# Weights of layer 2 in a ring of 12 entries, and the groups of layer 1's Strassen rounds in pairs

## The chip, the cores and the metric

The kernel runs on one core of a Trainium2 chip. The metric is device time in microseconds of one execution, the median of several runs. The engines are named as the profile names them: PE (matrix multiply) with its weight loads PEld, DVE (VectorE), ACT (ScalarE), POOL (GpSimd) and SP (SyncE, which here only issues DMAs, in program order, from one queue).

## The reference

Three stages follow one another: a masked linear attention with decay ("retention"), a first feed-forward layer with the activation mish, and a second one with a sigmoid form of gelu. The weights arrive in float64.

```python
ret = scores * Dmat[None, :, :, :]          # scores = q k^T / sqrt(64), Dmat: gamma ** (i - j), lower triangle
attn_out = np.matmul(ret, v)                # 4 batches, 8 heads, 576 positions, 64 wide
x = attn_out.transpose(0, 2, 1, 3).reshape(2304, 512)
h = x @ w_in                                # 512 x 2048
x = (h * np.tanh(softplus(h))) @ w_out      # layer 1: mish, 2048 x 512
h = x @ moe2_w_in
x = (h / (1.0 + np.exp(-1.702 * h))) @ moe2_w_out   # layer 2
```

## The kernel before

**Numbers.** Each float32 operand of a product is split into a high part that PE multiplies in one pass and a rest, and three products (high by high, high by rest, rest by high: `PARTS`) are added in PSUM. Weights arrive as float64 and are rebuilt with integer operations on DVE, ACT and POOL.

**Stages.** X holds the 2304 tokens as 512 x 2304 (four pieces of 128 partitions, 9 KB each). The attention fills X. `first_layer` works on blocks of 768 tokens: the first block (512 + 256 tokens) plainly, blocks 1 and 2 (`R_ROUNDS`) by Strassen's scheme in its up product (7 products instead of 8 of 2 x 2 quarters) and plainly in its down product. `second_layer` works on the three blocks (s = 0, 1, 2) with Strassen's scheme in both products. For one block of layer 2 there are 56 steps up (8 groups r of hidden units, 7 products each, `L645`) and 56 steps down (7 products, 8 r each, `L692`). A step is six matmuls of 128 x 384 columns.

**The weights of layer 2.** Before use, seven combinations of a quarter's weights are formed and written to DRAM, as the tensor `stream`. This is `prepare`: it loads a quarter's float64 words (`cr<-w_dram`), rebuilds and combines them in steps that are laid between PE's steps, and writes `stream<-cy` (`L328`). There are 32 preparations: 14 and 13 of them in the two Strassen blocks of layer 1, and the last five (j = 27 to 31, "late") in the first 56 steps of layer 2. Layer 2 then reads `stream` back, 112 steps for each of three blocks, 256 KB a step, into a ring of buffers:

```python
RING = [("w0", 4)] + [(f"x{k}", 2) for k in range(2)]
```

So the ring has one piece of 4 steps (w0, one DMA of 1 MB) and two of 2 steps (x0, x1, one DMA of 512 KB each): 8 entries. `load_weights(j + 2)` stands at the first step of piece j, on SP. The buffer that it fills is that of piece j - 1, so SP waits there until PE has done with piece j - 1. The buffers x2 and x3 hold the words of the late preparations, and temporaries (`t3` in x3, `u4` in x2).

**Operands of the down product.** For step i + 3 the function `operand`, called in step i, has ACT copy a piece to its high part and DVE subtract the rest, into a tile `g2`. Of four steps one used the buffer "side", the others a ring of 3 under the name "g", so four operands exist at a time.

**A Strassen round of layer 1.** Group r of a block is a list of 15 places, `R_STEPS`. At a number, PE does the six matmuls (`L1099`) of that product; at `None` it does one piece of the down product of the group before (`L1036`: `drawn`, 3 matmuls of 512 and 3 of 256 columns, one of four output pieces e). Products 1, 6, 5 and 3 use PSUM bank A, and 2, 7 and 4 bank E; ACT and DVE read a bank between two products (`pre`, `plus`), form mish and split the result (`high`, `low`). At each place, moved-on steps of the preparations under way are issued (`position`). 16 rounds are done. The ring here (`first_ring`) has the same shape, w0, x0, x1, and reads `first_stream` (`L981`).

**What sets the order.** `tc.manual_schedule()` keeps the written order on each engine. Every engine works off its own list in order, and waits on semaphores.

Of the kernel before, what the change touches and what calls it, by code (L numbers as in the profile page):

```python
# [82 lines left out]
R_STEPS = (1, None, 2, None, 6, None, 7, None, 5, None, None, 3, None, 4, None)  # L83
# [17 lines left out]
def retention_mish_gelu_kernel(ctx: ExitStack, tc: tile.TileContext, qkv, w1, w2, first_unit, rests, out):  # L101
# [55 lines left out]
    prepared = set()  # L157
    temp = []
# [115 lines left out]
    def prepare(j, r, part, half):  # L274
# [4 lines left out]
        raw = keep.tile([P, 4, P], I64, tag=f"x{2 + j % 2}", name="cr")  # L279
# [46 lines left out]
        yield from pause(2)  # L326
# [6 lines left out]
        yield from pause(2)  # L333
# [122 lines left out]
    def x_parts(s, t3_in=None):  # L456
# [3 lines left out]
        t3 = (place(t3_in) if t3_in else keep).tile([P, 2, TH], F32, tag=f"w{t3_in}" if t3_in else "x3", name="t3")  # L460
# [11 lines left out]
    def x_ops_in_turn(s, minus, t3_in=None):  # L472
# [6 lines left out]
        for jobs in (  # L479
            (lambda: high(1, x11), lambda: tt(nc.vector, t3, x22, x12, ALU.subtract)),  # L480
            (lambda: low(1, x11), lambda: high(2, x21)),
            (lambda: tt(nc.vector, x12, x12, x11, ALU.subtract),),
            (lambda: low(2, x21),),
            (lambda: tt(nc.vector, x11, t3, x11, ALU.add), lambda: high(6, x11)),
            (t_4, lambda: high(7, t3)),
            (lambda: low(6, x11),),
# [4 lines left out]
            (lambda: low(3, x22),),  # L491
            (lambda: high(4, x21),),
# [39 lines left out]
    RING = [("w0", 4)] + [(f"x{k}", 2) for k in range(2)]  # L532
# [51 lines left out]
    def second_layer():  # L584
# [12 lines left out]
        ops = {}  # L597

        def operand(i):
# [23 lines left out]
        for s in range(N_ROUND):  # L623
# [45 lines left out]
            assert len(prepared) == 4 * NR and not under_way  # L669
            extra = {}  # L670
# [30 lines left out]
            for n_p, p in enumerate(DOWN_ORDER):  # L701
# [21 lines left out]
                for e in range(2):  # L723
# [262 lines left out]
    def first_layer():  # L986
# [35 lines left out]
        pieces += [old(n - 3, range(NK))] + [old(n - 2, (e,)) for e in range(NK)] + [old(n - 1, (e, e + 1)) for e in (0, 2)]  # L1022
# [3 lines left out]
        def drawn(g, m, e, base):  # L1026
            def piece():
                if m == 0 and e == 0:
# [5 lines left out]
                for t, (o, w) in enumerate(BLOCKS):  # L1034
                    for a, b in PARTS:
                        nc.tensor.matmul(  # L1036
                            acc[t, e][:, :w],
                            lhsT=W[1, m // 2][:, m % 2, a, e * P : (e + 1) * P],
                            rhs=g[:, b, o : o + w],
# [4 lines left out]
                if m == NM - 1:  # L1044
                    for t, (o, w) in enumerate(BLOCKS):
                        evacuate(e, t, base + o)
# [3 lines left out]
        for n_s, s in enumerate(R_ROUNDS):  # L1050
            base = two(s)[0].start
            for r in range(NR):
# [30 lines left out]
                for n_e, p in enumerate(R_STEPS):  # L1083
                    if p is None:
                        if pieces:
                            pieces.pop(0)()
# [142 lines left out]
```

## Time and profile before

| | |
|---|---|
| median of 3 runs | 875.09 us (873.03 to 880.24) |
| the profiled execution | 875.2 us, of which 873.5 us lie between first and last instruction |
| PE busy | 821.9 us (94%) |
| PEld, DVE, ACT, POOL busy | 766.0, 608.9, 455.7, 110.4 us |
| DMA | 219.67 MB, mean 251 GB/s |
| layer 2 on PE | 465.4 to 869.9 us |

The span runs from the first instruction to the last one; 1.7 us of the execution lie around it. Busy time of PE counts each matmul to its modelled end, though the next one begins before that, so a PE that is busy 94% still has idle time that is to be found in the views of waits, chains and stretches.

### The profile page before, as it was taken

Reading aid. Unit: us, or ns where it says so; the run is one execution under the profiler, and the core shown is the slowest. Engines: PE = TensorE matmul, PEld = TensorE weight load, DVE = VectorE, ACT = ScalarE, POOL = GpSimd, SP = SyncE. Lnnn points to the kernel's source line nnn. Section 1 sums busy time; section 2 is a strip of 40 time slices with the busy share of each in tenths; the row PEclk is TensorE's granted clock in tenths of the full one; section 3 lists DMA queues with packets and bytes.
Section 4 is the critical chain, followed back from the end, with each engine's and each line's share of the span. In section 5 each row is a group of like instructions: output and inputs, shape, how many; then the busy total and the mean of one; then the engine's idle time right before and its main releaser. Section 6 shows DMA issues by size and latency. Waiting matters only on the chain.

```text
span 873.5 us, 14230 instructions
## 1 busy us (share of the span) xinstructions
PE 821.9 (94%) x5392; PEld 766.0 (88%) x5392; DVE 608.9 (70%) x1118; ACT 455.7 (52%) x861; POOL 110.4 (13%) x124
## 2 busy tenths in 40 slices
PE   8999999999999999998999889899889998999987
PEld 8898888888998999988999789898889988989987
DVE  4887999987767676676564676886345886445675
ACT  5446777757666566565563444652224563224542
POOL 3542322311221201221100110000000000000000
PEclk9999999999999999999999999999999999999999
DMA  9965668747979866979744788768576677676675
GB/s 365 424 280 178 227 212 253 253 142 256 342 256 350 289 201 207 311 261 319 279 143 163 290 314 277 247 227 269 195 243 214 219 260 266 202 249 224 209 265 178
DMA packets 84117, 219.67 MB, mean 251 GB/s; under 512 B 5584, under 2 KB 51664, under 8 KB 74960
## 3 DMA queue, kind: packets, MB, share of 16 engines
q1 hardware_dynamic: 83904, 218.56, 72.1%
q8 instruction: 43, 0.70, 0.3%
q14 instruction: 26, 0.21, 0.1%
q10 hardware_dynamic: 144, 0.20, 0.1%
HBM read 169.98 MB, written 48.76 MB: 250 GB/s over the span
## 4 chain that ended last, share of the span: by engine, by line
PE 58%; DMA 30%; DVE 4%; ACT 3%; issue 3%; POOL 1%; SPq 0%; POOLq 0%; DVEq 0%; ACTq 0%
DMA ring<-stream 22%; PE p L645 12%; PE p L692 11%; PE acc L1036 10%; PE p L1099 8%; PE h L389 8%; PE acc L410 7%; DMA unit<-qkv_dram 2%; DMA cr<-w_dram 2%; DMA ring<-first_stream 2%; DMA stream<-cy 2%; PE o L896 1%; PE sc L834 1%; PE o L885 1%; ACT c L122 1%
## 5 line engine op out<-in xcount | busy, mean ns | idle before, releaser
L645 PE MATMUL p<-xop,ring 128*128 128x384 f32 x1008 | 185.2, 342 | 21.9 <-DMA ring<-stream 21.1
L645 PEld LDWEIGHTS p<-xop,ring 128*128 128x128 f32 x1008 | 178.5, 192 | 28.3 <-DMA ring<-stream 13.5
L692 PE MATMUL p<-g,ring 128*128 128x384 f32 x1008 | 180.5, 336 | 17.0 <-DMA ring<-stream 16.3
L692 PEld LDWEIGHTS p<-g,ring 128*128 128x128 f32 x1008 | 173.9, 188 | 23.6 <-ACT g L122 16.5
L1036 PE MATMUL acc<-g,w 128*128 128x512 f32 (+1 forms) x768 | 152.1, 338 | 0.0
L1036 PEld LDWEIGHTS acc<-g,w 128*128 128x128 f32 x768 | 130.3, 188 | 18.3 <-ACT X L122 0.6
L1099 PE MATMUL p<-xop,ring 128*128 128x384 f32 x672 | 139.1, 342 | 4.7 <-DMA ring<-first_stream 3.7
L122 ACT ACTIVATE g<-cs 128x384 fp32r<-128x384 f32 x168 | 88.2, 525 | 83.7 <-PE p L692 83.6
L448 DVE TENSOR_TENSOR g<-cs,g 128x384 fp32r<-128x384 f32 x168 | 93.6, 557 | 45.5 <-ACT g L122 44.6
L1099 PEld LDWEIGHTS p<-xop,ring 128*128 128x128 f32 x672 | 114.1, 189 | 7.3 <-ACT cy L122 3.0
L122 ACT ACTIVATE cs<-cs 128x384 f32<-128x384 f32 x72 | 37.8, 524 | 128.8 <-DVE cs L448 125.3
L206 POOL TENSOR_TENSOR cy<-cr 128x256 int32<-128x256 int32 x64 | 48.2, 773 | 284.5 <-DVE cr L202 108.7
L410 PE MATMUL acc<-g,w 128*128 128x512 f32 (+1 forms) x384 | 72.6, 337 | 0.0
L410 PEld LDWEIGHTS acc<-g,w 128*128 128x128 f32 x384 | 60.3, 190 | 7.6
L448 DVE TENSOR_TENSOR g<-c,g 128x384 fp32r<-128x384 f32 x64 | 36.1, 567 | 41.7 <-ACT g L122 41.3
L122 ACT ACTIVATE g<-c 128x384 fp32r<-128x384 f32 (+1 forms) x96 | 50.3, 524 | 12.4 <-PE acc L410 10.3
L448 DVE TENSOR_TENSOR cs<-cs 128x384 f32<-128x384 f32 x96 | 54.0, 562 | 0.8
L206 POOL TENSOR_TENSOR raw<-raw 128x512 int32<-128x512 int32 x32 | 38.0, 1187 | 101.3 <-DVE raw L202 84.0
L122 ACT ACTIVATE raw<-raw 128x512 int32<-128x512 uint32 x64 | 41.8, 679 | 14.1 <-DVE raw L190 14.0
L122 ACT ACTIVATE cr<-cr 128x512 int32<-128x512 uint32 x64 | 42.0, 670 | 13.2 <-DMA cr<-w_dram 11.1
L122 ACT ACTIVATE c<-c 128x384 f32<-128x384 f32 x48 | 25.1, 524 | 41.9 <-DVE c L448 41.7
L122 ACT ACTIVATE c<-p 128x384 f32<-128x384 f32 x64 | 30.9, 483 | 29.8 <-PE p L1099 29.6
(79 smaller groups left out, 925.5 us busy)
## 6 DMA issues: line engine op xcount, KB each, us to landing
ring<-stream SPq DMA_DIRECT2D x42, 1024.0 KB, 4.8
ring<-stream SPq DMA_DIRECT2D x84, 512.0 KB, 4.5
stream<-cy SPq DMA_DIRECT2D x32, 896.0 KB, 5.3
raw<-w_dram SPq DMA_DIRECT2D x32, 512.0 KB, 7.9
cr<-w_dram SPq DMA_DIRECT2D x32, 512.0 KB, 5.1
unit<-qkv_dram SPq DMA_DIRECT2D x15, 1024.0 KB, 10.6
ring<-first_stream SPq DMA_DIRECT2D x14, 1024.0 KB, 6.7
ring<-first_stream SPq DMA_DIRECT2D x28, 512.0 KB, 6.0
```

The costliest lines, as they stand in the source:

```text
L122: nc.scalar.activation(out=o, in_=i, func=f, scale=scale, bias=bias)
L206: nc.gpsimd.tensor_tensor(out=o, in0=upper, in1=bits, op=ALU.add)
L389: nc.tensor.matmul(h[:, :n], lhsT=W[0, m // 2][:, m % 2, a, k * P : (k + 1) * P], rhs=xs[t, k][:, b, :n], start=((k, a, b) == order[0]), s ...
L410: nc.tensor.matmul(acc[t, e][:, :n], lhsT=W[1, m // 2][:, m % 2, a, e * P : (e + 1) * P], rhs=g[:, b, :n],  start=(begins(i) and a == 0 an ...
L448: eng.tensor_tensor(out=o, in0=a, in1=b, op=op)
L645: nc.tensor.matmul(banks[p], lhsT=w[:, k, a * P : (a + 1) * P], rhs=x[:, b, k], start=(p not in SAME and k == 0 and a == 0 and b == 0), st ...
L692: nc.tensor.matmul(banks[e, p], lhsT=w[:, e, a * P : (a + 1) * P], rhs=g[:, b], start=(p != 2 and r == 0 and a == 0 and b == 0), stop=(r = ...
L834: nc.tensor.matmul(sc[j][:n, p, :n], lhsT=kt[sl, p, :], rhs=qt[sl, p, :], start=True, stop=True)
L885: nc.tensor.matmul(o[sl, p, :n], lhsT=before[:, p, sl], rhs=qt[:, p, :], start=(p == 0), stop=True, skip_group_check=True,)
L896: nc.tensor.matmul(o[sl, p, :n], lhsT=v[:n, p * P + 64 * j : p * P + 64 * j + 64], rhs=pm[u][j][:n, p, :n], start=(c == 0 and p == 0), sto ...
L1036: nc.tensor.matmul(acc[t, e][:, :w], lhsT=W[1, m // 2][:, m % 2, a, e * P : (e + 1) * P], rhs=g[:, b, o : o + w], start=(m == 0 and a == 0 ...
L1099: nc.tensor.matmul(bank, lhsT=w[:, a, k * P : (k + 1) * P], rhs=x[:, b, k], start=(p in (1, 2, 7) and k == 0 and a == 0 and b == 0), stop= ...
```

## The change

It has five parts.

1. The ring of layer 2 takes x2 and x3 as well: pieces of 4, 2, 2, 2, 2 steps, 12 entries. `load_weights(j + 4)` stands at the first step of piece j; four pieces are loaded ahead of layer 2.
2. The words of the late preparations go into a tile `raws` of two halves in the buffer "side"; after the up steps of block 0 that buffer holds `t3` and `u4` (`spare`). In every preparation the write to `stream` stands one place later, and the place after it, where its buffer counts as free, one earlier.
3. The operands of the down product lie in pairs in the three buffers "g": six at a time.
4. `R_STEPS` puts the products of a round together in pairs, and a down piece takes two output pieces e: 6 matmuls of 512 columns, then 6 of 256. An empty place issues nothing on PE.
5. The steps of ACT and DVE in a round, and those that form the operands of the next block, are moved to fit.

```diff
-R_STEPS = (1, None, 2, None, 6, None, 7, None, 5, None, None, 3, None, 4, None)
+R_STEPS = (1, "down", "", 2, 6, "down", "", 7, 5, "down", "", 3, 4, "down", "")
...
+    spare, raws = [], []
...
-        raw = keep.tile([P, 4, P], I64, tag=f"x{2 + j % 2}", name="cr")
+        if j == sum(PREPARED_IN[:2]):
+            raws.append(keep.tile([P, 2, 4, P], I64, tag="side", name="raws"))
+        raw = raws[0][:, j % 2] if raws else keep.tile([P, 4, P], I64, tag=f"x{2 + j % 2}", name="cr")
         nc.sync.dma_start(out=raw, in_=w2[r, part, half])
...
-        yield from pause(2)
+        yield from pause(3)
         c, step = (r * NP, 1) if part == 0 else (UP_STEPS + r, NR)
         nc.sync.dma_start(
             out=stream[:, c : c + (NP - 1) * step + 1 : step, half],
...
-        yield from pause(2)
+        yield "skip"
         live["cy"] -= 1
...
+        if spare:
+            t3 = spare[0][:, :2]
...
-    RING = [("w0", 4)] + [(f"x{k}", 2) for k in range(2)]
+    RING = [("w0", 4)] + [(f"x{k}", 2) for k in range(NK)]
...
-            if i % 4:
-                g = keep.tile([P, 2, TH], F32R, tag="g", name="g2", bufs=LAG)
-            else:
-                g = keep.tile([P, 2, TH], F32R, tag="side", name="g2")
-            ops[i] = g
+            if c == UP_STEPS or i % 2 == 0:
+                twos[0] = keep.tile([P, 2, 2, TH], F32R, tag="g", name="g2", bufs=LAG)
+            g = ops[i] = twos[0][:, i % 2]
...
+            if s == 0:
+                spare.append(keep.tile([P, 4, TH], F32, tag="side", name="spare"))
...
-                            sums["u4"] = keep.tile([P, 2, TH], F32, tag="x2", name="u4")
+                            sums["u4"] = spare[0][:, 2:]
...
-        def drawn(g, m, e, base):
+        def drawn(g, m, es, base):
...
+                    for e in es:
+                        for a, b in PARTS:
+                            nc.tensor.matmul(
+                                acc[t, e][:, :w],
...
-                    elif n_e == 2:
+                    elif n_e == 3:
                         plus(11, E)
...
-                    pieces += [drawn(g_[h], 2 * r + h, e, base) for e in range(NK)]
+                    pieces += [drawn(g_[h], 2 * r + h, (e, e + 1), base) for e in (0, 2)]
```

On SP, at the start of layer 2, a load of 128x2048 is a w0 piece (4 steps), one of 128x1024 an x piece (2 steps). Ahead of the words of the first late preparation (`cr`, later `raws`) stand, before:

```order
L549 DMA ring<-stream 128x2048
L549 DMA ring<-stream 128x1024 x2
L280 DMA cr<-w_dram 128x512
L549 DMA ring<-stream 128x2048
L549 DMA ring<-stream 128x1024
L280 DMA cr<-w_dram 128x512
```

There three pieces of the ring (8 entries) come first. On the same queue at the same place, changed:

```order
L554 DMA ring<-stream 128x2048
L554 DMA ring<-stream 128x1024 x4
L283 DMA raws<-w_dram 128x512
L554 DMA ring<-stream 128x2048
L554 DMA ring<-stream 128x1024
L283 DMA raws<-w_dram 128x512
```

In the second list all five pieces stand ahead of the first words, and every later w0 load is followed by four x loads instead of two.

On SP a little later, around the second and third writes of late preparations (`stream<-cy`), before:

```order
L328 DMA stream<-cy 128x7x256
L280 DMA cr<-w_dram 128x512
L549 DMA ring<-stream 128x2048
L549 DMA ring<-stream 128x1024 x2
L328 DMA stream<-cy 128x7x256
L549 DMA ring<-stream 128x2048
```

Each of the two writes stands ahead of a w0 load. The same place, changed:

```order
L283 DMA raws<-w_dram 128x512
L331 DMA stream<-cy 128x7x256
L554 DMA ring<-stream 128x2048
L554 DMA ring<-stream 128x1024 x2
L331 DMA stream<-cy 128x7x256
L554 DMA ring<-stream 128x1024 x2
L554 DMA ring<-stream 128x2048
```

The second write still stands just ahead of a w0 load; behind the third, two x loads now come first.

On PE, between two Strassen rounds of layer 1 (`p` is a Strassen product, `acc` the down product of the group before), before:

```order
L1099 MATMUL p<-xop,ring 128x384 x6
L1036 MATMUL acc<-g,w_1236 128x512 x3
L1036 MATMUL acc<-g,w_1236 128x256 x3
L1099 MATMUL p<-xop,ring 128x384 x6
L1036 MATMUL acc<-g,w_1408 128x512 x3
L1036 MATMUL acc<-g,w_1408 128x256 x3
```

Products and down pieces take turns, six matmuls each. On PE at the same place, changed:

```order
L1105 MATMUL p<-xop,ring 128x384 x12
L1042 MATMUL acc<-g,w_1236 128x512 x6
L1042 MATMUL acc<-g,w_1236 128x256 x6
L1105 MATMUL p<-xop,ring 128x384 x6
L1042 MATMUL acc<-g,w_1408 128x512 x6
L1042 MATMUL acc<-g,w_1408 128x256 x6
```

Products 3 and 4 stand together, then a double down piece, and product 1 of the next group stands alone.

## Rows read from the trace of the kernel before

**Rows 1.** The view of waits, PE: us in total, times, longest.

```profile
PE p L645 <- DMA ring<-stream: 21.1, 19, 3.8
PE p L692 <- DMA ring<-stream: 16.3, 21, 1.0
PE p L1099 <- DMA ring<-first_stream: 3.7, 2, 2.8
```

**Rows 2.** View by stretches, all of layer 2: stretch, length, busy, clock, DMA share.

```profile
465.40:869.90 404.50, 365.67 (x2018) 352.30 (x2016) 257.69 (x481) 171.49 (x332) 6.24 (x10) 0.99 0.70 241
```

**Rows 3.** The chain of waits, 556 to 577 us: start, us, what.

```profile
557.32 4.41 PE p L692 x24
...
561.75 4.75 DMA ring<-stream
...
566.64 4.41 PE p L692 x24
```

**Rows 4.** Timeline of PE, 486 to 513 us: start, duration, what, count, idle time before.

```profile
485.77 6.58 PE L645 MATMUL p<-xop,ring 128*128 128x384 f32 x37
496.10 9.93 PE L645 MATMUL p<-xop,ring 128*128 128x384 f32 x48 [3.75 <-DMA ring<-stream]
```

**Rows 5.** The page's costliest groups: busy us, mean ns; idle before, releaser.

```profile
L692 PE MATMUL p<-g,ring 128*128 128x384 f32 x1008 | 180.5, 336 | 17.0 <-DMA ring<-stream 16.3
L122 ACT ACTIVATE g<-cs 128x384 fp32r<-128x384 f32 x168 | 88.2, 525 | 83.7 <-PE p L692 83.6
```

**Rows 6.** Timeline of PE, 556.5 to 568 us.

```profile
557.32 8.56 PE L692 MATMUL p<-g,ring 128*128 128x384 f32 x48 [0.71 <-DMA ring<-stream]
```

**Rows 7.** View by stretches: 56 steps each; the last columns are clock, DMA share, GB/s.

```profile
465.40:538.60 73.20, 63.35 (x339) 60.88 (x337) 47.32 (x97) 31.19 (x61) 6.24 (x10) 0.95 0.78 282
538.60:604.20 65.60, 60.19 (x337) 57.91 (x337) 50.30 (x92) 34.96 (x65) 0.00 (x0) 1.00 0.71 243
604.20:672.80 68.60, 61.70 (x336) 59.57 (x337) 33.19 (x61) 20.27 (x43) 0.00 (x0) 0.98 0.65 221
```

**Rows 8.** Clock after the wait that ended at 496.10 us, by stretches.

```profile
495.60:499.10 3.50, 3.00 (x10) 3.03 (x11) 0.67 (x2) 0.00 (x0) 0.00 (x0) 0.51 0.94 383
```

**Rows 9.** Line 549, SP's loads of layer 2's ring, from issue to landing.

```profile
DMA to landing us min/median/max: 3.5/4.7/7.3
```

**Rows 10.** DMA view, 465.4 to 538.6 us: GB/s in 40 slices.

```profile
GB/s 9 0 31 300 396 401 304 40 273 405 419 300 9 350 263 389 398 421 112 102 340 335 419 389 356 383 111 76 354 385 337 284 281 342 367 376 410 154 273 383
```

**Rows 11.** Timeline of SP, 486 to 512 us: issues.

```profile
491.63 1.09 SPq L549 DMA_DIRECT2D ring<-stream  x2
500.57 0.37 SPq L328 DMA_DIRECT2D stream<-cy  x1
...
501.89 4.48 SPq L549 DMA_DIRECT2D ring<-stream  x3
```

**Rows 12.** The chain of waits, 486 to 512 us.

```profile
488.78 7.18 DMA ring<-stream
...
501.89 7.04 DMA ring<-stream
```

**Rows 13.** View by stretches, about 8 steps: length, PE, PEld, DVE, ACT busy.

```profile
585.40:595.00 9.60, 8.61 (x49) 8.32 (x49) 8.39 (x18) 4.21 (x8) 0.00 (x0) 1.00 0.72 239
```

**Rows 14.** Timeline of PE in one round of layer 1, 302 to 319 us.

```profile
302.39 2.26 PE L1036 MATMUL acc<-g,w 128*128 128x512 f32 x12
304.48 1.21 PE L1099 MATMUL p<-xop,ring 128*128 128x384 f32 x6
...
318.24 0.98 PE L1036 MATMUL acc<-g,w 128*128 128x512 f32 x4
```

**Rows 15.** The chain of waits, 382 to 404 us.

```profile
389.62 1.00 DVE cy L325
...
392.13 8.39 DMA ring<-first_stream
```

**Rows 16.** The view of waits, PE, 197 to 465.4 us.

```profile
PE p L1099 <- DVE c L448: 0.5, 2, 0.3
```

More of the change, by code (lines that the diff above doesn't have):

```diff
@@ L459, in x_parts @@
         x11, x12, x21, x22 = X[:, 0:2, t], X[:, 0:2, u], X[:, 2:4, t], X[:, 2:4, u]
-        t3 = (place(t3_in) if t3_in else keep).tile([P, 2, TH], F32, tag=f"w{t3_in}" if t3_in else "x3", name="t3")
+        if spare:
+            t3 = spare[0][:, :2]
+        else:
+            t3 = (place(t3_in) if t3_in else keep).tile([P, 2, TH], F32, tag=f"w{t3_in}" if t3_in else "x3", name="t3")
         def high(p, x):
@@ L1021, in first_layer @@
         n = BOTH
-        pieces += [old(n - 3, range(NK))] + [old(n - 2, (e,)) for e in range(NK)] + [old(n - 1, (e, e + 1)) for e in (0, 2)]
+        pieces += [old(n - 3, range(NK)), old(n - 2, (0, 1)), old(n - 2, (2, 3)), old(n - 1, range(NK))]
         unit_of = {first: j for j, (first, _) in enumerate(first_units)}
         tick = [BOTH]
-        def drawn(g, m, e, base):
+        def drawn(g, m, es, base):
             def piece():
-                if m == 0 and e == 0:
+                if m == 0 and es[0] == 0:
                     for q in range(NK):
@@ L1034, in piece @@
                 for t, (o, w) in enumerate(BLOCKS):
[L1035 to L1039, printed above, removed]
-                            start=(m == 0 and a == 0 and b == 0 and not (t == SIDE and e % 2)),
-                            stop=(m == NM - 1 and a == 1),
-                            skip_group_check=True,
-                        )
+                    for e in es:
+                        for a, b in PARTS:
+                            nc.tensor.matmul(
+                                acc[t, e][:, :w],
+                                lhsT=W[1, m // 2][:, m % 2, a, e * P : (e + 1) * P],
+                                rhs=g[:, b, o : o + w],
+                                start=(m == 0 and a == 0 and b == 0 and not (t == SIDE and e % 2)),
+                                stop=(m == NM - 1 and a == 1),
+                                skip_group_check=True,
+                            )
                 if m == NM - 1:
-                    for t, (o, w) in enumerate(BLOCKS):
-                        evacuate(e, t, base + o)
+                    for e in es:
+                        for t, (o, w) in enumerate(BLOCKS):
+                            evacuate(e, t, base + o)
             return piece
@@ L1083, in first_layer @@
                 for n_e, p in enumerate(R_STEPS):
-                    if p is None:
-                        if pieces:
-                            pieces.pop(0)()
-                    else:
+                    if p == "down":
+                        pieces.pop(0)()
+                    elif p:
                         i = n_s * UP_STEPS + r * NP + R_ORDER.index(p)
@@ L1143, in first_layer @@
                         for name in ("skip", "pool", "act early", "vector"):
[L1144 removed]
+                            if name != "act early" or n_e not in (6, 7):
                                 position(name, now)
                 for h in range(2):
[L1147 removed]
+                    pieces += [drawn(g_[h], 2 * r + h, (e, e + 1), base) for e in (0, 2)]
                 if n_s == 1 and r == NR - 1:
```

24 lines of the change are left out of this document (11 added, 13 removed).

## The prediction

> **What bounds the kernel now.** I read the view of waits first, PE alone: of the 873.5 - 821.9 = 51.6 us in which PE is idle (the table above), 37.4 us end when a piece of layer 2's weights lands (21.1 us in 19 waits in the up steps, 16.3 us in 21 in the down steps), against 3.7 us in two waits for layer 1's weights [rows 1]. So the place is layer 2, and the view by stretches gives its length: 404.5 us from its first matmul to the end of its last, at a DMA share of only 0.70 [rows 2]. DMA is not short on average; it is late. The chain of waits says why. In the steady part it repeats one pattern: 24 matmuls of PE, 4.41 us, beside one load of 4.75 us, and round again every 9.32 us [rows 3]. 24 matmuls are four steps, those of x0 and x1. The load is that of the 4-step piece w0: it is issued when PE leaves w0, and PE needs it four steps later. Four steps are shorter than the load, so PE waits once in eight steps, 42 times in 336 steps.
>
> What would layer 2 take without waits? 37 matmuls in a row took 6.58 us [rows 4]; the last one's modelled time of 0.33 us [rows 5] taken off, 36 intervals take 6.25 us, or 0.174 us a matmul and 1.04 us a step. 2016 matmuls take 350.8 us. Layer 2 is therefore 404.5 - 350.8 = 53.7 us longer than its matmuls. That is more than the 37.4 us of the waits view, for two reasons that a reader can check. Each wait hides up to 0.336 - 0.174 = 0.16 us under the modelled end of the matmul before it: 40 waits, 6.5 us. And after three long waits PE's clock is granted at half, 1.2 instead of 2.4 GHz: the clock stands at 0.51 after the wait of 3.75 us [rows 8], and 48 matmuls then take 9.93 us [rows 4] instead of 8.56 us [rows 6], 1.4 us lost each time; the clock of 0.95 and 0.98 in the first and the third stretch [rows 7] is that of two such dips and of one. What remains of the 53.7 us are the slower first matmuls behind each wait.
>
> **The change, part by part.**
>
> The ring. After it, w0's load is issued at the same moment and needed after four x pieces, eight steps or 8.35 us; an x load is needed after ten steps, 10.4 us. The loads of layer 2 land after 3.5 us at the least, 4.7 in the median and 7.3 at the most [rows 9]. The lead exceeds the worst of them, so all 42 waits go where the DMA stays as fast as that: -53.7 us, the dips with them, since they follow long waits. Nothing is added on any engine: the same bytes in 28 loads of 1 MB and 112 of 512 KB instead of 42 and 84. The first load into x3 waits for DVE's last use of `t3`; ten steps cover it, and without cover it would cost one landing, 4.7 us.
>
> What is late next: bandwidth. In the first 56 steps the last five preparations run beside the ring. That stretch has 73.2 us and a DMA share of 0.78 [rows 7], 57.1 us of DMA work; PE's 56 steps are 58.4 us. It fits with 1 us to spare, so any hole in the queue is lost. The other stretches carry 0.71 x 65.6 = 46.6 us and 0.65 x 68.6 = 44.6 us [rows 7] and have room.
>
> Against this the Trainium skill can be held, "DMA: Bandwidth & Descriptors", "Where 436 GB/s comes from": between HBM and SBUF the HBM side binds at about 358 GB/s for a core. The stretch moves 20.6 MB (282 GB/s x 73.2 us), which at that rate would be an estimated 57.7 us, again just under PE's time. But the slices of that stretch reach 405, 419 and 421 GB/s [rows 10], so the trace does not show such a limit, and the sum goes by the shares.
>
> The second thing that can be late is SP, which issues in order. The write of a late preparation waits on DVE, and the w0 load stands behind it, as in the order of the change. In the trace SP issues nothing from 492.7 to 500.57 us, where the write leaves, and the w0 load leaves at 501.89 [rows 11], 1.3 us later; it lands after 7.04 us, the one before after 7.18 [rows 12]. That write belongs to step 26, twelve matmuls behind 496.10 us, which PE, most of them at half speed, began at about 499.5 us: it was 1.1 us behind PE. In the changed order it belongs to step 27; if it leaves 1.1 us after that step begins, the load leaves 1.3 us later, 1.4 us into step 28; 7.1 us more makes 8.5 us, against the 8.35 us of lead: PE waits 0.15 us. But DVE had the 3.75 us of PE's wait [rows 4] to catch up, and without that it may be as much later: 3.9 us. Between the two lie 2 us, and the shares above leave 0.5 us more for holes in the queue: +2.5 us. Bounds: 0, and 9 us if the stretch stays bound by DMA at a share of 0.85 (57.1 / 0.85 = 67.2 us), which is far from what the rows give.
>
> Operands in pairs. ACT waits 83.6 us for PE in layer 2, for a free buffer [rows 5]. With six operands instead of four the buffer for step i + 3 was last read by step i - 2 or earlier instead of i - 1, so those waits mostly go, and DVE's behind them. This costs nothing and moves no end by itself; it matters because DVE becomes tight. Near the end of the down steps DVE is busy 8.39 us in eight steps [rows 13], and eight steps will take 8.35 us instead of 9.3. The surrounding groups leave it some room (50.3 of 58.4 us over that stretch [rows 7], counting overlaps twice) and the operands are three steps ahead. Bounds 0 and 1 us for each of the two stretches with this load; I take +1 us together. For the rest of layer 2, the late loads of a whole run, +0.5 us.
>
> Layer 1. One round took from 302.39 to 318.24 us, 15.85 us for 15 groups of 2304 columns, 1.057 us each; 12 down matmuls in a row took 304.48 - 302.39 = 2.09 us, 1.045 a group [rows 14]. Taking turns thus costs 0.012 x 15 = 0.18 us a round at most. About half of the turns go: 16 rounds x 0.09 = 1.5 us gained. Bounds 0 and 2.9.
>
> The late weights of layer 1 (3.7 us idle [rows 1], and a dip behind the longer wait, 1.4 us as above) come from SP too: the load is issued at 392.13 us, after DVE's last step of a preparation at 389.62 to 390.62 [rows 15], and lands 8.4 us later. In the changed order the same write still stands ahead of the same load, but DVE's step stands one place earlier. Bounds: all 5.1 us gone, or as much again; I take -1.5 us.
>
> `raws` and `spare` are other addresses for the same work: 0. If the words of two late preparations got in each other's way there, the write after them would be late by one landing, and it is counted in the bounds of the first stretch.
>
> Sum, against the profiled execution's own 875.2 us (the median, 875.09, is the same): 875.2 - 53.7 + 2.5 + 1 + 0.5 - 1.5 - 1.5 = **822.5 us**.
>
> **The rivals.**
>
> *DVE becomes the bound in the down steps* of blocks 0 and 1. For it: 8.39 us of work in 8.35 us, in order, with waits for ACT between. Then those two stretches keep their 65.6 us instead of 58.4: +14.4 us less the 1 us counted, 836 us. Against it: DVE's waits are for ACT, ACT's are for buffers, and those are what the pairs free.
>
> *DMA becomes the bound in the first 56 steps*: 67.2 instead of 58.4 + 2.5 us, +6.3, 829 us. For it: 57.1 us of transfers in 58.4. Against it: twelve entries are full when the stretch begins, and the work of DMA is not tied to one step.
>
> *The ring is deeper only in name*: SP holds the loads back behind writes, outputs and waits for PE so that w0 still comes late, and half of the waits stay: 822.5 + 53.7 / 2 = 849 us. Against it: in the steady part SP issues the w0 load at the moment PE leaves the piece (557.32 + 4.41 = 561.73, and the load at 561.75 [rows 3]), with nothing ahead of it.
>
> *Slower: layer 1 stalls in each round.* In a pair such as 7 and 5, then down, 3 and 4, ACT and DVE must take 22 out of both banks between the end of 5 and the start of 4; that was four groups (4.2 us) and is three (3.15 us). ACT and DVE also carry the preparations. From the point at which this takes 3.15 + 3.3 = 6.5 us in all 16 rounds, 16 x 3.3 = 53 us of the gain are lost; at 7 us a round loses 3.85 and the time is 822.5 + 62 = 884 us. Against it: today PE waits for DVE's `c` only 0.5 us in all [rows 16].
>
> **How the numbers follow.** Forecast 0.72, DVE 0.11, DMA 0.10, ring in name only 0.04, slower 0.03. The forecast's own range runs from 875.2 - 53.7 - 2.9 - 5.1 = 813.5 (no new wait, all of layer 1's gone) to about 829; to hold 8 in 10 it is carried to the DMA and the DVE case, 838. The two cases beyond it hold 0.07. About 1% is what a measurement of this kernel can tell from no change (the three runs spread over 0.8%): faster by more is all but the slower case, 0.96; a milder form of that one would end within 1%, 0.01; slower 0.03.
>
> **What would show it.** In the waits view ring<-stream should fall from 37.4 us to under 6, with what is left in the first stretch. The chain should be PE alone over most of layer 2, the whole of which should take 352 to 357 us, each later stretch 58.3 to 59.5 us with the clock at 1.00, the first about 61. ACT's wait of 83.6 us should shrink. Layer 1's rounds should take 15.8 us. The forecast is wrong if stretches stay at 65 us with PE waiting on DVE or ACT, if the DMA share of the first stretch stays near 0.8 while PE waits, or if layer 1 shows waits of PE for `c`.

## The result, and the profile after

The changed kernel takes 851.54 us (median of four runs, 851.22 to 853.28), the kernel before 877.66 us beside it (873.03 to 882.93): a ratio of 0.9705 (95% interval 0.9641 to 0.9768). It is faster, but by about half of what was forecast, and it lies 13.5 us above the upper end of the range. The profiled execution took 853.28 us, its span 851.6.

The view by stretches of the changed kernel says in two rows where the forecast held and where it did not. Its columns are stretch, length, busy time of PE, PEld, DVE, ACT and POOL, clock, DMA share, GB/s. The first row is all rounds of layer 1, from the first matmul of a round to the first of layer 2; the second is all of layer 2; the next two are the first 56 steps of layer 2 and the second, the last row with 340 matmuls in place of 336:

```profile
197.70:491.70 294.00, 266.99 (x1478) 244.04 (x1476) 181.76 (x363) 161.79 (x293) 37.69 (x54) 0.97 0.73 244
491.70:848.00 356.30, 350.95 (x2018) 349.06 (x2016) 248.41 (x481) 161.81 (x333) 5.94 (x10) 1.00 0.80 271
491.70:556.60 64.90, 59.58 (x338) 58.01 (x337) 45.30 (x95) 30.80 (x60) 5.94 (x10) 1.00 0.87 307
556.60:615.20 58.60, 58.60 (x340) 58.60 (x339) 48.13 (x94) 32.28 (x67) 0.00 (x0) 1.00 0.82 279
```

Layer 2 fell from 404.5 us [rows 2] to 356.3, where 352 to 357 was forecast, and in the second stretch PE is busy without a gap at full clock, where it took 65.6 us before [rows 7]. The rounds of layer 1 rose. Their row in the kernel before is this one:

```profile
197.40:465.40 268.00, 263.30 (x1477) 242.21 (x1476) 183.63 (x363) 161.67 (x295) 41.92 (x54) 0.99 0.77 264
```

That is 26.0 us more. 22.3 us of them are new idle time of PE (294.0 - 267.0 = 27.0 against 268.0 - 263.3 = 4.7); the other 3.7 us are a longer busy time for the same matmuls, at a mean clock of 0.97 instead of 0.99. PE's busy tenths in the 40 slices of the changed kernel's page, 21.3 us each, show the holes. The 6, the 7 and the next 6 lie between 234 and 405 us; layer 2, about the last 17 slices, has no such hole:

```profile
PE   8999999999969979996989998999999999999998
```

The view of waits of PE, changed kernel (us in total, times, longest):

```profile
PE p L1105 <- DVE c L451: 22.5, 7, 7.1
PE p L648 <- DVE cs L451: 3.5, 2, 1.8
PE acc L1042 <- DVE g L451: 2.5, 3, 1.8
...
PE p L648 <- ACT s L122: 1.7, 1, 1.7
...
PE p L1105 <- DMA ring<-first_stream: 1.1, 1, 1.1
```

The 37.4 us for layer 2's weights [rows 1] are gone entirely. In their place stand seven waits of PE in layer 1 for DVE's `c`, the step that reads a product out of the bank that PE wants next; they were 0.5 us before [rows 16]. DVE is not busier there (181.8 us against 183.6), so it was itself waiting. The view of waits of DVE in the rounds says for what. In the kernel before:

```profile
DVE cr L190 <- DMA cr<-w_dram: 12.6, 11, 3.2
DVE cy L316 <- POOL cy L206: 7.2, 5, 2.7
```

In the changed kernel, the same view:

```profile
DVE cy L319 <- POOL cy L207: 39.0, 19, 4.8
DVE cr L191 <- DMA cr<-w_dram: 18.2, 13, 2.2
```

DVE waits for POOL's `join` of a preparation (it puts the words together into the result buffer `cy`), and POOL has only 37.7 us of work in 294. The chain of waits of the changed kernel from 363 to 393 us shows what POOL waits for. Its summary line comes first, then start, us, what:

```profile
by line: DMA stream<-cy 69.8%; POOL cy L207 15.1%; DVE cy L319 6.7%; PE p L1105 4.4%; issue 4.3%; DVE c L451 1.6%; SPq L283 1.1%; DVE cy L320 1.0%; POOLq L207 0.5%; SPq L331 0.1%
...
363.83 6.34 DMA stream<-cy
...
370.40 1.20 POOL cy L207 x2
371.61 0.33 SPq L283
...
372.04 6.55 DMA stream<-cy
...
380.88 8.03 DMA stream<-cy
...
389.07 1.19 POOL cy L207 x2
390.28 0.30 DVE cy L319
...
391.43 0.48 DVE c L451
...
391.95 1.33 PE p L1105 x3
```

For 30 us the chain is a write to `stream`, a join, the next write, and so on, with PE at 4%; in the first turn shown the load of words stands between the join and the write. The timeline of SP in the changed kernel shows the loop closing (start, duration, what):

```profile
380.01 0.33 SPq L283 DMA_DIRECT2D cr<-w_dram  x1
380.44 0.38 SPq L986 DMA_DIRECT2D ring<-first_stream  x1
380.88 0.42 SPq L331 DMA_DIRECT2D stream<-cy  x1
390.28 0.33 SPq L283 DMA_DIRECT2D cr<-w_dram  x1
390.70 0.39 SPq L331 DMA_DIRECT2D stream<-cy  x1
```

And the timeline of DVE, POOL and PE beside it:

```profile
384.46 1.08 DVE L328 TENSOR_TENSOR cy<-cy 128x896 fp32r<-128x896 f32 x1
...
389.07 1.18 POOL L207 TENSOR_TENSOR cy<-cr 128x256 int32<-128x256 int32 x2 [9.08 <-DMA stream<-cy]
390.28 0.82 DVE L319 TENSOR_TENSOR cy<-cy 128x128 f32<-128x128 f32 x3 [4.74 <-POOL cy L207]
391.35 0.55 DVE L451 TENSOR_TENSOR c<-p,c 128x384 f32<-128x384 f32 x1
391.95 1.33 PE L1105 MATMUL p<-xop,ring 128*128 128x384 f32 x3 [7.07 <-DVE c L451]
```

Read it backwards. DVE finished the last step of a preparation at 385.54 us (L328), but its write leaves only at 390.70. It stands on SP behind a load of words (`cr`, L283), and that load waits until the words of an earlier preparation have been joined. The join waits 9.08 us for the result buffer, which is free when the write before has landed: 380.88 + 8.03 = 388.91. Join, load and write then follow within 1.8 us, and the next write holds up the next join in the same way. There are two result buffers (`cy`) and two of words (`cr`), so a write that stands behind the load three preparations later cannot leave before its predecessor has landed. The four writes shown leave at 363.83, 372.04, 380.88 and 390.70, 9.0 us apart; in the kernel before the eleven writes from 345.94 to 418.49 us are 7.3 us apart in the mean (timeline of SP). There a write leaves as soon as its result is finished. In the chain of waits of the kernel before from 340 to 392 us DVE's last step (L325) ends at 358.74, and the write is issued at 358.80:

```profile
357.73 1.01 DVE cy L325
358.80 6.75 DMA stream<-cy
```

In the changed kernel the write shown above leaves 5.2 us after its result. Over 26 of the 27 writes of the rounds the time between the end of DVE's last step and the issue of the write adds up to 1.7 us in the kernel before and to 44.1 us in the changed one (from the starts and durations of these instructions in the two traces; the last write of the first block is left out, which is 13.2 us late in the changed kernel behind loads of the ring and not behind the load three preparations on).

The backlog reaches PE through DVE's order: the preparation's step L319 waits 4.74 us, and `c` stands behind it. In the stretch 389.80 to 397.00 us, after PE's wait of 7.07 us, the clock is granted at 0.53, the lower of its two levels.

SP's own waits in the rounds show the turn most plainly. In the kernel before:

```profile
SPq L328 <- DVE cy L325: 89.3, 26, 8.4
...
SPq L280 <- POOL cy L206: 28.2, 17, 4.3
```

In the changed kernel:

```profile
SPq L283 <- POOL cy L207: 87.1, 23, 8.0
...
SPq L331 <- DVE cy L328: 42.3, 9, 9.8
```

Before, SP stood at a write and waited for DVE; now it stands at a load and waits for POOL, with the finished write behind it.

### The profile page after: what moved, and what is told of

Same layout as the page of the kernel before. It is cut to its first block, busy times and chain, and to the rows that moved or that the text cites. A ratio compares the mean times of both kernels' runs of the same rounds, so it can differ in the third digit from the quotient of the medians.

```text
span 851.6 us, 14187 instructions
## 1 busy us (share of the span) xinstructions
PE 810.9 (95%) x5392; PEld 764.8 (90%) x5392; DVE 597.8 (70%) x1118; ACT 446.3 (52%) x861; POOL 105.9 (12%) x124
## 4 chain that ended last, share of the span: by engine, by line
PE 69%; DMA 16%; DVE 6%; POOL 3%; issue 2%; ACT 2%; SPq 0%; POOLq 0%; DVEq 0%
PE p L697 21%; PE p L648 17%; DMA stream<-cy 11%; PE h L392 8%; PE acc L413 7%; PE acc L1042 7%; PE p L1105 6%; POOL cy L207 2%; DMA unit<-qkv_dram 2%; DMA cr<-w_dram 1%; DVE cy L319 1%; PE o L901 1%; DMA raws<-w_dram 1%; PE sc L839 1%; DVE g L451 1%
## 5 line engine op out<-in xcount | busy, mean ns | idle before, releaser
L648 PE MATMUL p<-xop,ring 128*128 128x384 f32 x1008 | 176.6, 335 | 5.3 <-DVE cs L451 3.5
L697 PE MATMUL p<-g,ring 128*128 128x384 f32 x1008 | 175.2, 334 | 0.0
L1105 PE MATMUL p<-xop,ring 128*128 128x384 f32 x672 | 132.8, 342 | 24.5 <-DVE c L451 22.5
L1042 PE MATMUL acc<-g,w 128*128 128x512 f32 (+1 forms) x768 | 147.8, 342 | 2.5 <-DVE g L451 2.5
L1042 PEld LDWEIGHTS acc<-g,w 128*128 128x128 f32 x768 | 126.8, 191 | 21.4 <-DVE g L451 4.1
L122 ACT ACTIVATE g<-cs 128x384 fp32r<-128x384 f32 x168 | 79.0, 517 | 60.2 <-PE p L697 60.0
L451 DVE TENSOR_TENSOR g<-cs,g 128x384 fp32r<-128x384 f32 x168 | 90.0, 554 | 26.7 <-ACT g L122 25.1
L122 ACT ACTIVATE cs<-cs 128x384 f32<-128x384 f32 x72 | 37.7, 524 | 106.1 <-DVE cs L451 106.0
L413 PE MATMUL acc<-g,w 128*128 128x512 f32 (+1 forms) x384 | 72.3, 337 | 0.0
L413 PEld LDWEIGHTS acc<-g,w 128*128 128x128 f32 x384 | 60.2, 190 | 7.6
L207 POOL TENSOR_TENSOR cy<-cr 128x256 int32<-128x256 int32 x54 | 37.7, 718 | 231.7 <-DVE cr L203 83.0
L122 ACT ACTIVATE cy<-cy 128x896 fp32r<-128x896 f32 (+1 forms) x40 | 38.8, 969 | 30.1 <-DVE cy L320 23.7
L319 DVE TENSOR_TENSOR cy<-cy 128x128 f32<-128x128 f32 x96 | 25.1, 289 | 40.3 <-POOL cy L207 39.2
```

The source lines that it names most:

```text
L122: nc.scalar.activation(out=o, in_=i, func=f, scale=scale, bias=bias)
L207: nc.gpsimd.tensor_tensor(out=o, in0=upper, in1=bits, op=ALU.add)
L319: nc.vector.tensor_tensor(out=v[:, o], in0=v[:, a], in1=v[:, b], op=op)
L413: nc.tensor.matmul(acc[t, e][:, :n], lhsT=W[1, m // 2][:, m % 2, a, e * P : (e + 1) * P], rhs=g[:, b, :n],  start=(begins(i) and a == 0 an ...
L451: eng.tensor_tensor(out=o, in0=a, in1=b, op=op)
L648: nc.tensor.matmul(banks[p], lhsT=w[:, k, a * P : (a + 1) * P], rhs=x[:, b, k], start=(p not in SAME and k == 0 and a == 0 and b == 0), st ...
```

## The experiments

Theory A is that loop: the write, one place later, now stands on SP behind a load that waits, by way of POOL, for the write before. Theory B, the rival, is the one named in the prediction: products in pairs leave ACT and DVE too little time between two groups. Theory C, added for the last two runs, is that the first runs of the changed kernel came from a slower occasion. The kernel before took 865.6 to 869.2 us beside the experiments, so ratios to it are what is compared. Theory A has a count: how many of the 32 writes stand, in SP's order, behind the load of words of the preparation three later. It is 6 in the kernel before and 18 in the changed one. In every kernel below that moves the write on SP, the place at which its result buffer counts as free is the same, four places behind DVE's last step: 2 + 2, 3 + 1, 1 + 3 or 4 + 0. Part 2 of the change, which has it one place earlier, is wrong there, and so is the expectation of e1; in the traces of the changed kernel, e1 and e10, and of e4, e11 and e12, the lists of PE, DVE, ACT and POOL are the same, and only SP's differ.

**e1: the pauses put back**, all else as changed.

```diff
-        yield from pause(3)
+        yield from pause(2)
...
-        yield "skip"
+        yield from pause(2)
```

> The changed kernel with the two old pauses in every preparation (write to the stream one place earlier, its buffer free one place later); rounds, ring and pairs stay. In the changed kernel 18 of 32 writes stand on SP behind the load of the words three preparations on, which waits for POOL, which waits for an earlier write to land; before it was 6, here it is 12, in shorter rows. Theory A (order on SP, a closed loop of about 8.2 us per preparation against 6.9 us of schedule): the 26 us that layer 1's rounds have become longer shrink by a third to two thirds, 834 to 843 us. Theory B (the products in pairs leave ACT and DVE too little time for the banks): nothing changes, 849 to 854 us.

Measured: 832.73 us, ratio 0.9598 [0.9532, 0.9664]; rounds 275.8 us. 12 writes stand behind the load. 18.2 of the 26.0 us that the rounds had lost go with the pauses alone, a little more than the two thirds that theory A allowed; the time lies 1.3 us below its range. Theory B, which expected no change, does not fit.

**e3: the old rounds**, with the new pauses (`R_STEPS`, drawn pieces and `n_e` as before).

```diff
-R_STEPS = (1, "down", "", 2, 6, "down", "", 7, 5, "down", "", 3, 4, "down", "")
+R_STEPS = (1, None, 2, None, 6, None, 7, None, 5, None, None, 3, None, 4, None)
```

> The changed kernel with the old rounds of layer 1 (products and down pieces one by one); the new pauses, the ring of 12 and the pairs of operands stay. 13 of 32 writes stand behind the load. Theory A: part of the loss stays, 832 to 843 us. Theory B: all of layer 1's loss goes, 824 to 829 us.

Measured: 838.72 us, ratio 0.968 [0.9618, 0.9743]; rounds 276.8 us, 13 writes behind the load. The old rounds bring back 17.2 of the 26.0 us, about as much as the old pauses; taken by itself e3, inside theory A's range, says that a loss stays without any pairs.

**e4: the kernel before with the ring of 12 entries**, `raws`, `spare` and the operands in pairs, but old rounds and old pauses.

```diff
-    RING = [("w0", 4)] + [(f"x{k}", 2) for k in range(2)]
+    RING = [("w0", 4)] + [(f"x{k}", 2) for k in range(NK)]
...
```

> The kernel before with the ring of 12, the words of late preparations and the temporaries in the side buffer, and the operands in pairs; old pauses, old rounds. 6 of 32 writes stand behind the load, as before. Both theories: layer 1 as before (268 us from 197 to 465 us), layer 2 as in the changed kernel (356 us instead of 404.5), so 875 - 48 = 827 us, 823 to 831. If it stays above 835, layer 2's gain was paid for by something in layer 1 that neither theory has.

Measured: 824.56 us, ratio 0.9516 [0.9461, 0.9572]; rounds 271.2, layer 2 354.9 us. Layer 2 has the length that the prediction's terms make (350.8 + 2.5 + 1 + 0.5 = 354.8), with the old rounds and the old pauses.

**e6: the load of words up to three places later**, so that no write stands behind the load three preparations on.

```diff
+        late_by = 0
+        while j > len(prepared) + 2 and late_by < 3:
+            late_by += 1
+            yield "skip"
...
-        yield from pause(4)
+        yield from pause(4 - late_by)
```

> The changed kernel, in which a load of words is issued up to three places later, so that no write stands behind the load three preparations on (0 of 32); the steps after it keep their places. Rounds, pauses, ring and pairs are the changed kernel's. Theory A: the loop is open, layer 1's rounds return to 264 to 270 us, 822 to 830 us. Theory B: nothing changes, 849 to 854 us. A wait of DVE for words that now land later could cost up to 1 us a preparation in either.

Measured: 843.71 us, ratio 0.9728 [0.9669, 0.9788]; rounds 281.1 us. The loop is open, since DVE's wait for POOL fell from 39.0 to 2.9 us, but the time lies outside both ranges. The writes keep their places behind the loads of layer 1's weights, so it was not those that made DVE wait. The edit made a wait of its own: the words, loaded later, are not there when DVE wants them. The view of waits of DVE in the rounds of this kernel:

```profile
DVE cr L191 <- DMA cr<-w_dram: 45.3, 16, 5.9
```

These waits were 18.2 us in the changed kernel. So e6 speaks for the loop in its waits and decides nothing by its time.

**e5: the changed kernel with the writes issued by ACT**, and **e8: the same in e4**, as its control.

```diff
-        nc.sync.dma_start(
+        nc.scalar.dma_start(
             out=stream[:, c : c + (NP - 1) * step + 1 : step, half],
```

> The changed kernel with the writes to the stream issued by ACT instead of SP; nothing else differs, and the loads of words keep their early places. Theory A, sharpened (in the changed order a finished result cannot be written, since SP stands at the next load of words, which waits for POOL, which waits for the last write to land): a write leaves when DVE has finished it, DVE's waits for POOL in the rounds fall from 39 us to under 10, its waits for words stay at 18 instead of the 45 of the run with the later loads, and the rounds take 266 to 274 us instead of 294: 823 to 831 us. Theory B (pairs of products leave too little time): 845 to 853 us.

> The kernel with the ring alone (old rounds, old pauses) with the writes issued by ACT. There only 6 of 32 writes stand behind the load, so theory A leaves little to gain: 821 to 827 us, against 824.6 of the ring alone. If ACT pays for the issue or holds its own work behind a write, it is slower than that by up to 5 us, and the run with the changed rounds carries the same cost.

Measured: e5 862.41 us, ratio 0.9937 [0.9893, 0.9982]; e8 851.25 us, ratio 0.9809 [0.9748, 0.987]. Both missed. In e5 DVE's wait for POOL did not fall under 10 us, as theory A had it, but rose to 46.3, and the rounds took 300.2 us. Its premise did not hold: on ACT's list the write stands three places behind DVE's last step among ACT's own work, and the same 26 writes left 45.9 us in all after their results, as late as in the changed kernel (44.1). So e5 does not open what it was to open. The control shows a cost of the move besides: e8 takes some 27 us more than e4 (851.25 against 824.56), 13.0 of them in the rounds and 11.6 in layer 2. Its writes land after 3.8, 6.1 and 13.0 us (least, median, most), in e4 after 3.8, 5.5 and 8.1. The Trainium skill, "DMA: Bandwidth & Descriptors", "Issuing engines are not separate DMA queues", says that initiating DMAs from several engines only saves the issuing sequencer's time; here it saved nothing that counts. What made the landings longer is not shown.

**e10: the write two places earlier**, its buffer counted free at the same place as in the changed kernel. Only SP's order differs from that kernel's; ring, rounds and pairs are the same.

```diff
-        yield from pause(3)
+        yield from pause(1)
...
-        yield "skip"
+        yield from pause(3)
```

> The changed kernel with the write of a preparation two places earlier, one place behind DVE's last step; its buffer is free at the same place as in the changed kernel, so every other instruction keeps its place and only SP's list differs: 4 of 32 writes stand behind the load three preparations on, not 18. Theory A (the place of the write on SP): DVE's waits for POOL in the rounds fall from 39 us to under 12, the rounds from 294 to 266 to 275 us, the whole to 822 to 832 us. Theory B (products in pairs): 845 to 853 us. In between, 833 to 844, both hold a part.

Measured: 825.65 us, ratio 0.9519 [0.9469, 0.957]; 4 writes behind the load. The view by stretches of e10, its rounds and its layer 2:

```profile
195.80:465.90 270.10, 260.25 (x1478) 239.93 (x1477) 180.86 (x363) 161.97 (x293) 39.18 (x54) 1.00 0.76 265
465.90:820.80 354.90, 350.63 (x2018) 349.07 (x2016) 249.30 (x482) 161.90 (x333) 7.04 (x10) 1.00 0.77 272
```

The view of waits of DVE in these rounds:

```profile
DVE cr L191 <- DMA cr<-w_dram: 29.3, 11, 4.4
DVE cy L319 <- POOL cy L207: 5.5, 8, 1.2
```

All of this lies inside theory A's ranges. The pairs of products are all still there, and the stall is not: theory B falls.

**e11: e4 with the write two places later**, and **e12: e4 with it one place earlier**. Neither has pairs of products.

```diff
-        yield from pause(2)
+        yield from pause(4)
...
-        yield from pause(2)
+        yield from pause(0)
```

(e12 has 1 and 3 in these two places.)

> The ring alone (old rounds), with the write two places later than in the kernel before and its buffer free at the same place as there: only SP's list differs, and 23 of 32 writes stand behind the load, more than in the changed kernel. Theory A: the rounds become as slow as the changed kernel's without any pair of products, 285 to 300 us instead of 271, the whole 838 to 855 us. Theory B: as the ring alone, 823 to 828 us.

> The ring alone (old rounds), with the write one place earlier than in the kernel before: 2 of 32 writes stand behind the load instead of 6. Theory A: a little less waiting than the ring alone, rounds 266 to 271 us, the whole 820 to 825 us. Theory B: as the ring alone, 823 to 828 us. If SP's earlier wait for DVE holds up loads of weights, 826 to 832 us.

Measured: e11 878.9 us, ratio 1.0121 [1.0077, 1.0164], 23 writes behind the load; e12 827.81 us, ratio 0.9533 [0.9498, 0.9568], 2 writes. Late writes without any pairs make the rounds 46.2 us longer than in e4 and the whole 1.2% longer than the kernel before, although layer 2 takes 361.2 us, 43.3 less than there. Theory A had the direction right and the size wrong: the rounds lie 17 us above its range. Of the 46.2 us 31.0 are idle time of PE and 15.2 a longer busy time for the same matmuls, at a clock of 0.94. e12 lies 3 us above theory A's range and inside theory B's: with 6 writes behind the load there was nothing left to gain. The view by stretches of e11, its rounds:

```profile
195.70:513.00 317.30, 279.30 (x1477) 254.99 (x1476) 180.59 (x363) 161.68 (x295) 34.68 (x54) 0.94 0.68 226
```

The view of waits of DVE in them:

```profile
DVE cy L319 <- POOL cy L207: 70.1, 18, 8.5
```

**e13 and e14: the changed kernel and e10 once more, on one chip**, five rounds each, because their first times came from different occasions.

> The changed kernel itself again, unedited, beside e14 and the kernel before on one chip. In the experiments' batches the kernel before took 865.6 to 868.9 us, where it took 877.66 beside the first runs of the changed kernel, so 851.54 us can't be set beside 825.65 directly. Theory A (the write behind the load of words closes a loop that is paced by the landing of a write): the loss stays here, since the loop is in SP's order: rounds of layer 1 285 to 296 us, DVE waiting 25 to 40 us for POOL's cy, a ratio of 0.967 to 0.985. If the first runs were slow because of their chip alone (theory C): rounds 268 to 274 us, DVE's wait for POOL under 10 us, a ratio of 0.950 to 0.955, as in e10.

> The kernel of e10 again beside e13 on one chip: the write two places earlier. Theory A: rounds 268 to 273 us, ratio 0.949 to 0.957, 15 to 27 us less than e13. Theory C: the same time as e13 within 1%.

Measured: e13 854.31 us, ratio 0.9804 [0.9755, 0.9853]; e14 826.26 us, ratio 0.9502 [0.9456, 0.9548]. Two edited lines, which move one DMA on one queue, are worth 28 us on one chip, 1 us more than theory A allowed. The rounds in the view by stretches of e13:

```profile
195.80:489.90 294.10, 267.25 (x1477) 244.55 (x1476) 181.39 (x363) 162.02 (x293) 36.63 (x54) 0.97 0.72 244
```

The same of e14:

```profile
197.40:464.90 267.50, 260.18 (x1478) 239.79 (x1477) 180.90 (x363) 162.33 (x293) 38.22 (x54) 1.00 0.76 268
```

The changed kernel's rounds take 294 us again, and DVE waits 40.6 us for POOL in them, so theory C falls too. Theory A's ranges are missed by half a microsecond or so in two places, these 40.6 us and the 267.5 us of e14's rounds.

Set side by side, the kernels that issue their writes on SP and load their words where the kernel before does fall into one sequence, whichever rounds they have. The columns are the writes behind the load, the length of the rounds, DVE's wait for POOL in them, and the time by which the 26 writes leave later than DVE has finished the results, in us:

| kernel | rounds of products | writes behind | rounds, us | DVE <- POOL | writes late by |
|---|---|---|---|---|---|
| e12 | old | 2 | 271.4 | 3.2 | 1.7 |
| e10, e14 | pairs | 4 | 270.1, 267.5 | 5.5, 5.6 | 1.2, 1.2 |
| before, e4 | old | 6 | 268.0, 271.2 | 7.2, 6.7 | 1.7, 1.7 |
| e1 | pairs | 12 | 275.8 | 20.1 | 16.2 |
| e3 | old | 13 | 276.8 | 28.8 | 9.8 |
| the change, e13 | pairs | 18 | 294.0, 294.1 | 39.0, 40.6 | 44.1, 44.5 |
| e11 | old | 23 | 317.3 | 70.1 | 71.0 |

Up to six writes behind the load cost nothing: there no finished result waits, since the load has left before the result is ready. From there on the loss grows with the time that finished results wait: e3's rounds are 5.6 us longer than e4's, e1's 7.0 us longer than the mean of e10 and e14, the changed kernel's 25.2 longer than that mean, and e11's 46.2 longer than e4's.

**e7: the ring of the kernel before, 8 entries, in four pieces of two steps**, w0's buffer as two halves; and **e9: e4 with 10 entries**. These ask what in the ring made layer 2 faster, its size or its lead: how long before its use a piece is issued.

```diff
-    RING = [("w0", 4)] + [(f"x{k}", 2) for k in range(2)]
+    RING = [("w0", 2), ("w0b", 2)] + [(f"x{k}", 2) for k in range(2)]
...
```

> The kernel before with its ring of 8 entries in four pieces of two steps (w0's buffer in two halves, each loaded when it is free) instead of 4, 2, 2; nothing else. Lead theory (the 4-step piece is needed four steps after its load is issued, 4.2 us, and lands after 4.75): every piece now has six steps, 6.25 us, the one wait in eight steps goes, and only the long ones in the first 56 steps stay in part: layer 2 takes 357 to 366 us instead of 404.5, the whole about 40 us less than before. Depth theory (twelve entries are needed to even out the loads): half of the gain at most, layer 2 above 378 us.

> The ring alone with 10 entries (4, 2, 2, 2) instead of 12: w0 is needed six steps after its load, 6.25 us, against landings of 4.7 us in the median and 7.3 at the most. Lead theory: layer 2 takes 356 to 362 us (354.9 with 12 entries), and what is added stands in the first 56 steps; in all 825 to 832 us. Depth theory: more than 370 us.

Measured: e7 831.73 us, ratio 0.959 [0.9528, 0.9652]; e9 826.29 us, ratio 0.9526 [0.9464, 0.9587]. The view of waits of PE in e7, which has no buffer more than the kernel before:

```profile
PE p L652 <- DMA ring<-stream: 2.5, 5, 1.2
PE p L699 <- DMA ring<-stream: 1.4, 2, 1.2
```

37.4 us of waits become 3.9, and layer 2 takes 358.8 us. Cutting the 4-step piece in two lengthens its lead from four steps to six, 6.3 us against a landing of 4.7, and that is most of the gain. e9, where the w0 piece keeps its 1 MB and has six steps of lead as well, takes 357.2 us for layer 2. The two or four entries more, with the operands in pairs that e9 and e4 also have, are worth what is left, under 1%. In layer 2 both runs lie inside the ranges of the lead theory; as a whole e7 takes 33.9 us less than the kernel before beside it, where about 40 was expected. The Trainium skill, "DMA: Bandwidth & Descriptors", "Measured (HBM→SBUF, 128 partitions, SWDGE, issued from GpSimd)", has the rule to batch DMAs to at least 1 MiB for at least 75% of the peak rate. It speaks of bandwidth, on DMAs issued from GpSimd; here, issued from SP, smaller pieces lost nothing that shows, because the time had gone to lead and not to bandwidth. On the changed kernel's page a piece of 1 MB takes hardly longer to land than one of 512 KB (count, size, median us from issue to landing):

```profile
ring<-stream SPq DMA_DIRECT2D x112, 512.0 KB, 4.6
...
ring<-stream SPq DMA_DIRECT2D x28, 1024.0 KB, 4.8
```

## Why the prediction was half right

*The ring, -53.7 us: right.* All waits for the weights of layer 2 went (40 in [rows 1]; the prediction's 42 is 336 / 8), the dips of the clock in layer 2 with them, and from the second stretch on PE is busy throughout. e4 shows the same without the parts for layer 1.

*The first stretch, +2.5 us (bounds 0 and 9): within the bounds, mis-sized.* The stretch took 64.9 us, 6.5 more than its matmuls. It was not the weights that were late, as the step on SP had it: PE waited for DVE's `cs` and ACT's `s`, 5.2 us in three waits. Ahead of the first two, steps of the last preparations stand between on DVE's and ACT's lists. The third goes back to a `cs` that waited 2.1 us for a write to `stream` to land, 9.4 us after its issue at 538.09. With the loop gone the same stretch takes 63.5 us (e4, e10). DMA did not bind the loads: its share rose to 0.87 with 307 GB/s, and the rival priced at 829 us did not come.

*DVE in the down steps and late loads, +1 and +0.5: not needed.* The later stretches take 58.2 to 58.4 us each, with no wait of PE for DVE. ACT's wait for a free buffer shrank only from 83.6 us [rows 5] to 60.0, where the prediction had it mostly go; it cost nothing. The group of the changed kernel's page:

```profile
L122 ACT ACTIVATE g<-cs 128x384 fp32r<-128x384 f32 x168 | 79.0, 517 | 60.2 <-PE p L697 60.0
```

In all, layer 2 gave 48.2 us where the terms made 49.7. That they come so close is in part luck: the first stretch was sized 4.0 us too small, and the 1.5 us that were not needed made up for some of it.

*Fewer turns in layer 1, -1.5: not seen.* Rounds in pairs take 270.1 and 267.5 us (e10, e14), old rounds 271.2 and 271.4 (e4, e12). The difference is no larger than that between two runs of one kernel (270.1 and 267.5).

*The late weights of layer 1, -1.5 (bounds -5.1 and +5.1): here the prediction failed.* The term itself came: PE's waits for these weights fell from 3.7 us [rows 1] to 1.1, and to 1.0 in e10. What failed is the step that cleared the moved write. It read: "In the changed order the same write still stands ahead of the same load". It asked only what stands behind the moved write, loads of weights. It did not ask what now stands ahead of it: the load of words. That load waits for POOL, and POOL waits for the write before. The trace of the kernel before showed both halves: SP waits 28.2 us for POOL at the load, and POOL waits 85.9 us in 14 waits for a write to land, over the whole kernel. The changed order in layer 2, shown ahead of the prediction, even has a line of words directly above the line of the write. The moved write was given a price of at most 5.1 us in layer 1; it closed a loop with a landing in each turn. The rounds cost 26.0 us more, where the two terms for layer 1 made 3.0 less. With that and layer 2's 1.5 us the sum is 822.5 + 29.0 + 1.5 = 853.0 us, against a profiled 853.28.

*What the forecast itself was worth.* Without the loop the profiled spans are 824.9 us (e4), 824.3 (e10) and 823.1 (e14), where the sum makes 822.5 - 1.7 = 820.8. But the kernel before took 867.7 to 869.2 us beside these runs, not 875: as a ratio they gain 4.8 to 5.0%, where the forecast is 822.5 / 875.2, or 6.0%. There is no trace of the kernel before from there, so which of its parts was shorter stays open.

*The slower rival* named the right place, PE waiting for `c` in layer 1, with the wrong mechanism. It made the pairs responsible; e10 keeps them and is fast, e11 has none and is the slowest of all.

Not settled: how the lateness of the writes turns into the length of the rounds, 16.2 us into 7.0 in e1 and 44.1 into 25.2 in the changed kernel. Counts and lateness order the kernels, but no run breaks the sum down. A third result buffer, which might open the loop without moving the write, was not tried, and no run shows whether there is room for it.

Four kernels come out ahead of the changed one: e4 (ratio 0.9516 [0.9461, 0.9572]), e10 (0.9519 and, again, 0.9502 [0.9456, 0.9548]), e9 (0.9526) and e12 (0.9533). They can't be told apart.

## What to carry to other kernels

When an instruction is moved on a queue that issues in order, read what now stands ahead of it as well as what stands behind: if what stands ahead waits for a buffer that an earlier instruction of the same kind frees, the queue has become a loop, and its pace is a landing and not the schedule. A prefetch that is late although DMA has time to spare wants lead, and cutting the largest piece in two may give most of it without a buffer more. The waits of the issuing queue, which cost nothing by themselves, show such a turn first: look at which of its instructions waits, and for whom.

## What the runs showed of the hardware

With the writes issued from ACT's queue (e8) their longest landing was 13.0 us, where the same kernel with the writes on SP has 8.1 (e4), and the kernel was some 27 us slower; the cause was not looked for. Loads of 1 MB and of 512 KB, issued from SP among each other, landed after 4.8 and 4.6 us in the median in the changed kernel. PE's clock was granted at 0.53 in the stretch behind the wait of 7.07 us in the changed kernel, and stood at 1.00 over the rounds of e10, whose longest wait for `c` is 2.0 us.
